# Dense channel-weight conversion, a later priority and a VectorE subtraction in an attention and token-mixing kernel

## The chip, the cores and the metric

The kernel runs on one core of a Trainium2 chip. Its time is device microseconds (us) of one execution. The core has five engines, each with a queue of its own that it works off in order: TensorE (PE in the profile; its weight loads are PEld), VectorE (DVE), ScalarE (ACT), GpSimd (POOL) and SyncE (SP), which here only starts transfers. Matmuls write to PSUM, and GpSimd works on SBUF alone in this kernel. The granted clock (PEclk) is the share of its full clock that TensorE was given.

## The reference

Batch 8, 8 heads, 576 positions, 64 values a head, 128 features. First an attention without a softmax over positions:

```
def phi(x):
    proj = einsum('bhsd,df->bhsf', x, w_phi)
    proj = proj - max(abs(proj), axis=-1)
    return concatenate([exp(proj), exp(-proj)], axis=-1)
kv  = einsum('bhsf,bhsd->bhfd', phi(k), v)
z   = sum(phi(k), axis=2)
out = einsum('bhsf,bhfd->bhsd', phi(q), kv) / (einsum('bhsf,bhf->bhs', phi(q), z) + 1e-6)
```

Its result, with the heads side by side as 512 channels, is `x` of a mixer, in float64 because the four weights are float64:

```
u   = x + (relu(xT @ w_tok1) @ w_tok2)T
out = u + relu(u @ w_ch1) @ w_ch2          # w_ch1 512 x 1536, w_ch2 1536 x 512
```

The maximum is per position, over the 128 features, for each of the 8 x 8 x 576 keys and queries.

## The kernel before

Heads are worked in 32 pairs `i` (4 for each batch). Six kinds of work are written as Python generators and woven together by `weave`:

- `keys` (for each pair five groups of key blocks): the projection `pp`, the maximum `mx`, the difference `pm`, both exponentials `kp`, then the sums `pkv` on TensorE.
- `queries` (for each pair a tail and four pieces): the same up to `pm`, then `turn` transposes on TensorE (`pt`), takes exponentials `qf`, splits them into a high and a low part (`qh`, `ql`), and `numerators` multiplies with `kv` (`pn`), inverts the denominators (`den`, a reciprocal on VectorE) and scales `xt` on GpSimd.
- `token_stream`: for each batch and each half of its channels transposes `px`, splits `xh`, `xl`, products `pa`, relu and split `ah`, `al`, products `ph`, and the sum into `xt`.
- `load_weights`: all weights are float64 in memory. `convert` loads one block as 64-bit words (`raw`), builds a float32 of it (`bits`) and splits that into two float32r parts. This takes one ScalarE instruction (an absolute value, L131), four on VectorE (L132 to L135), a rounding on ScalarE (L72) and a subtraction on GpSimd (L75). The 24 blocks of 128 x 512 of the channel weights are called `bitsc` in the profile; c1_c_e stands for block c of w_ch1 from column e on, c2_k for rows k of w_ch2.
- `channel_stream`: blocks of 256 positions, 18 in all. Block `i` takes six up projections `h` (L81) with relu and split `gh`, `gl`, and six down projections `acc`. It can start when the batch's tokens are mixed, and waits for the weights that it needs.

Products are made with float32r parts, three matmuls each (`mm3`, L79 to L82), but for batch 0 (pairs 0 to 3, `i < PLAIN`) keys and queries go through TensorE as float32, each such matmul showing as two records. There `less_max` is called with `base` 64 for keys and 0 for queries, and reads the projection straight from PSUM.

For base 0 (batch 0's queries) the maximum is negated on VectorE (`nmx`, L230) and added on ScalarE while it copies (L232, once for each block of 128 positions); in all other cases one subtraction (L234) does it, on VectorE for base 64, on GpSimd else.

What sets the order: `weave` always takes the next step of the stream that is behind its share. A step yields its cost, divided by the stream's share; the cost of a channel weight comes from `pace`, 8.0 until the queries of batch 0 are written out (pair 3 in `attended`), and then 1.0. The order in which instructions are written out is their priority for a scheduler, which then orders each engine's queue by what it reckons to be ready first. Steps of keys and queries are put ahead in it by `tc.high_priority()`, from the moment at which batch 0's token mix has been written out (`mixed` is not empty).

Of the kernel before, what the change touches and what calls it, by code (L numbers as in the profile page):

```python
# [12 lines left out]
AF = mybir.ActivationFunctionType  # L13
ALU = mybir.AluOpType
# [3 lines left out]
P = 128  # L18
B, H, S, D = 8, 8, 576, 64
NP = H // 2  # L20
F = 128
# [3 lines left out]
NC_, NE, NT = C // P, E // P, T // P  # L25
# [17 lines left out]
def mixer_kernel(ctx, tc, qk, vm, vt, w_phi, w1, w2, wc1, wc2d, out):  # L43
    nc = tc.nc

    cst = ctx.enter_context(tc.tile_pool(name="cst", bufs=1))
    wk = ctx.enter_context(tc.tile_pool(name="wk", bufs=2))
# [17 lines left out]
    def column(pool, n, **kw):  # L65

        return pool.tile([P, 32], F32, **kw)[:, :n]
# [71 lines left out]
        return t.rearrange("p a b -> p (a b)")  # L139

    def pace():
        return 1.0 if NP - 1 in attended else 8.0

    def load_weights():
        for u in (0, 3):
# [45 lines left out]
    def less_max(ts, units, name, base=None):  # L191

        n, kind = len(units), name[0]
        if base == D:
            ps = ps_a.tile([P, 2, 2, F], F32, tag=f"a{nplain['k'] % 2}", name=f"pp{name}")
            nplain["k"] += 1
        elif base == 0 and (nplain["q"] % 2 == 0 or nplain["q"] >= BORROWED):
            ps = ps_h.tile([P, 2, 2, F], F32, tag="h", name=f"pp{name}")  # L200
            nplain["q"] += 1
        elif base == 0:
            ps = ps_w.tile([P, 2, 2, F], F32, tag="keys", name=f"pp{name}", bufs=1)
            nplain["q"] += 1
        elif kind == "k":
            ps = ps_w.tile([P, 2, 2, F], F32, tag="keys", name=f"pp{name}", bufs=1)
        else:
            ps = ps_w.tile([P, 2, 2, F], F32, name=f"pp{name}", **REST)
        for i, u in enumerate(units):
            t, c = (ts[1], 512) if u is None else (ts[u[0]], P * u[1])  # L210
            if base is None:
                nc.tensor.matmul(ps[:, i].rearrange("p two f -> p (two f)"), t[:, c:c + P],  # L212
                                 wp2.rearrange("p two f -> p (two f)"), start=True, stop=True)
            else:
                rows = slice(base, base + D)
                nc.tensor.matmul(ps[:, i, 0], t[rows, c:c + P], wp[rows], start=True, stop=True)
        if base is None:
            part = wk.tile([P, 2, F], F32, tag="part", name=f"part{name}")
            nc.scalar.copy(part[:, :n], ps[:, :n, 1])
            pr = wk.tile([P, 2, F], F32, tag="p", name=f"p{name}")  # L220
            nc.vector.tensor_tensor(pr[:, :n], ps[:, :n, 0], part[:, :n], op=ALU.add)
            pr, eng = pr[:, :n], nc.gpsimd
        else:
            pr, eng = ps[:, :n, 0], nc.vector
        mx = column(wk, 2, tag=f"mx{kind}", name=f"mx{name}")
        nc.vector.tensor_reduce(mx[:, :n], pr, axis=AX.X, op=ALU.max, apply_absolute_value=True)
        pm = wk.tile([P, 2, F], F32, tag=f"pm{kind}", name=f"pm{name}", bufs=1 if kind == "t" else 2)
        if base == 0:
            nmx = column(wk, 2, tag="nmx", name=f"nmx{name}")
            nc.vector.tensor_scalar(nmx[:, :n], mx[:, :n], -1.0, None, op0=ALU.mult)  # L230
            for i in range(n):
                nc.scalar.activation(pm[:, i], pr[:, i], AF.Identity, bias=nmx[:, i:i + 1])  # L232
        else:
            eng.tensor_tensor(pm[:, :n], pr, mx[:, :n].unsqueeze(2).to_broadcast([P, n, F]), op=ALU.subtract)  # L234
        return pm

    nplain = {"k": 0, "q": 0}
    raws, pairs, kvs, loaded = {}, {}, {}, set()
    asked, attended, mixed = set(), set(), set()
# [307 lines left out]
    def weave(streams):  # L547

        streams = [[g, share, urgent, 0.0] for g, share, urgent in streams]
        now = 0.0  # L550
        while streams:
            for s in sorted(streams, key=lambda s: s[3]) * 2:
                with tc.high_priority() if s[2] and mixed else nullcontext():
                    step = next(s[0], "end")
                if step is None:
                    continue
                now = max(now, s[3])
                if step == "end":
                    streams.remove(s)
                else:  # L560
                    s[3] = max(s[3], now - LAG) + max(step, 0.01) / s[1]
                break
            else:
                raise RuntimeError("every stream waits")

    weave([(keys(), 5.2, True), (queries(), 5.2, True), (token_stream(), 8.0, False),
           (load_weights(), 10.0, False), (channel_stream(), 19.5, False)])

# [41 lines left out]
```

## Time and profile before

| | |
|---|---|
| median of 3 runs | 1180.97 us (1180.92 to 1181.36) |
| span of the profiled execution | 1183.6 us, 2.6 us above that median |
| TensorE busy | 1137.6 us, 96% |
| VectorE busy | 867.1 us, 73% |
| ScalarE, GpSimd busy | 531.5 us, 587.1 us |
| mean granted clock | 0.975 |

The span of the profiled execution goes from its first to its last instruction, and no other time of that execution is given. Rows of the page are read by stage: slices of 29.6 us show in tenths how busy an engine is. A line number of a helper, such as L81 (a matmul), L74 and L75 (a split), covers many uses, so the names of the tiles tell what it is.

### The profile page before, as it was taken

To read this page: it belongs to the slowest core of one execution; us is meant where nothing else is said; L and a number is where in the kernel's file an instruction comes from. 1 tells how busy PE (TensorE), PEld (TensorE's weight loads), DVE (VectorE), ACT (ScalarE), POOL (GpSimd) and SP (SyncE) were. 2 spreads that over 40 slices of the span, in tenths; PEclk is the share of its full clock that TensorE was granted. 3 is DMA by queue.
4 is the path that set the end of the run, shared out by engine and by line. 5 is a ranking of instruction groups with operands and counts; after the bars stand their busy time and mean duration, and the time that the engine had idled before them with its cause. 6 is when DMAs were issued, how large, how long until landed. Compare 5 with 4: busy or idle time off the path is not lost.

```text
span 1183.6 us, 24087 instructions
## 1 busy us (share of the span) xinstructions
PE 1137.6 (96%) x9032; PEld 1102.0 (93%) x9032; DVE 867.1 (73%) x1782; ACT 531.5 (45%) x1545; POOL 587.1 (50%) x734
## 2 busy tenths in 40 slices
PE   8789897899999999999999999999999999999998
PEld 7667887898999999999999999999999999999998
DVE  7977899986777888887878677684787978763111
ACT  5767565453444445444444443343353544431110
POOL 3344775854555566465555455473564655431000
PEclk9679898999999999999999999999999999999999
DMA  9541222111111111111111011110111110000000
GB/s 232 150 135 28 72 84 71 50 31 28 31 40 32 49 31 32 49 32 49 32 34 46 20 31 49 30 50 1 49 31 49 32 48 12 19 1 19 19 19 19
DMA packets 65300, 54.31 MB, mean 46 GB/s; under 512 B 44768, under 2 KB 56416, under 8 KB 65184
## 3 DMA queue, kind: packets, MB, share of 16 engines
q1 hardware_dynamic: 63824, 52.41, 15.4%
q8 instruction: 72, 1.18, 0.4%
q10 hardware_dynamic: 1360, 0.36, 0.2%
q14 instruction: 44, 0.36, 0.1%
HBM read 43.32 MB, written 9.44 MB: 45 GB/s over the span
## 4 chain that ended last, share of the span: by engine, by line
PE 78%; DVE 11%; ACT 4%; issue 3%; POOL 2%; DMA 2%; SPq 0%; DVEq 0%; POOLq 0%; ACTq 0%
PE h L81 23%; PE acc L81 23%; PE pkv L300 8%; PE pn L81 7%; PE ph L81 3%; PE pa L81 3%; PE pt L356 3%; PE ppq L212 2%; PE ppk L212 2%; DVE qh L74 2%; PE pn L389 1%; DVE den L401 1%; PE px L423 1%; DMA rawc<-in_wc 1%; DVE bitsc L132 1%
## 5 line engine op out<-in xcount | busy, mean ns | idle before, releaser
L81 PE MATMUL acc<-gh,wc 128*128 128x256 f32 x1728 | 345.1, 283 | 0.0
L81 PEld LDWEIGHTS acc<-gh,wc 128*128 128x128 f32 x1728 | 276.0, 188 | 0.2 <-ACT gh L489 0.2
L81 PE MATMUL h<-uh,wc_h 128*128 128x256 f32 x864 | 246.8, 286 | 4.3 <-ACT wc_h L72 2.2
L81 PE MATMUL h<-uh,wc_l 128*128 128x256 f32 x864 | 245.9, 285 | 0.8 <-POOL wc_l L75 0.8
L81 PE MATMUL h<-ul,wc_h 128*128 128x256 f32 x864 | 243.9, 282 | 0.3 <-POOL ul L470 0.3
L81 PE MATMUL acc<-gl,wc 128*128 128x256 f32 x864 | 242.0, 282 | 0.6 <-DVE gl L490 0.6
L278 ACT ACTIVATE kp<-pmk 128x256 f32<-128x256 f32 (+1 forms) x320 | 109.2, 389 | 171.1 <-POOL pmk L234 168.1
L300 PE MATMUL pkv<-v,kp 128*128 128x65 f32 (+1 forms) x1152 | 165.7, 278 | 6.8 <-ACT kp L278 3.3
L81 PEld LDWEIGHTS h<-uh,wc_h 128*128 128x128 f32 x864 | 163.7, 190 | 5.8 <-ACT wc_h L72 2.6
L300 PEld LDWEIGHTS pkv<-v,kp 128*128 128x128 f32 x1152 | 155.9, 200 | 12.6 <-ACT kp L278 5.4
L75 POOL TENSOR_TENSOR ql<-qf,qh 128x320 fp32r<-128x320 f32 (+1 forms) x112 | 103.4, 923 | 127.7 <-DVE qh L74 110.8
L81 PEld LDWEIGHTS h<-uh,wc_l 128*128 128x128 f32 x864 | 163.4, 189 | 1.1 <-POOL wc_l L75 1.1
L81 PEld LDWEIGHTS h<-ul,wc_h 128*128 128x128 f32 x864 | 163.8, 190 | 0.5 <-POOL ul L470 0.5
L81 PEld LDWEIGHTS acc<-gl,wc 128*128 128x128 f32 x864 | 162.5, 188 | 0.7 <-DVE gl L490 0.7
L490 DVE SCALAR_TENSOR_TENSOR gl<-h,gh 128x512 fp32r<-128x512 f32 x108 | 73.5, 680 | 89.2 <-ACT gh L489 88.7
L74 DVE CAST qh<-qf 128x320 fp32r<-128x320 f32 (+1 forms) x224 | 106.5, 489 | 34.6 <-ACT qf L363 29.1
L401 DVE RECIPROCAL den<-den 128x320 f32<-128x320 f32 x64 | 124.6, 1947 | 3.2 <-ACT den L397 2.2
L363 ACT ACTIVATE qf<-pt 128x320 f32<-128x320 f32 (+1 forms) x256 | 92.6, 412 | 71.2 <-PE pt L356 68.5
L81 PE MATMUL pn<-qh,kv 128*128 128x320 f32 (+1 forms) x448 | 118.8, 302 | 3.5 <-DVE qh L74 1.5
L489 ACT ACTIVATE gh<-h 128x512 fp32r<-128x512 f32 x108 | 64.9, 601 | 116.0 <-PE h L81 115.2
L402 POOL TENSOR_TENSOR xt<-xt,den 128x320 f32<-128x320 f32 x64 | 53.7, 839 | 114.7 <-DVE den L401 87.8
L470 POOL TENSOR_TENSOR ul<-xt,uh 128x64 fp32r<-128x64 f32 (+3 forms) x120 | 62.2, 543 | 84.2 <-ACT uh L469 83.3
(110 smaller groups left out, 2415.3 us busy)
## 6 DMA issues: line engine op xcount, KB each, us to landing
raw<-in_qk SPq DMA_DIRECT2D x27, 576.0 KB, 3.7
rawc<-in_wc SPq DMA_DIRECT2D x24, 512.0 KB, 4.2
v<-in_vm SPq DMA_DIRECT2D x31, 256.0 KB, 3.3
out_x<-xt SPq DMA_DIRECT2D x12, 256.0 KB, 2.2
out_x<-xt SPq DMA_DIRECT2D x16, 192.0 KB, 2.0
raw<-in_w SPq DMA_DIRECT2D x8, 256.0 KB, 4.6
out_x<-xt SPq DMA_DIRECT2D x16, 128.0 KB, 1.9
pair<-in_qk SPq DMA_DIRECT2D x8, 160.0 KB, 4.7
```

Source lines behind the costliest of these rows:

```text
L74: eng_hi.tensor_copy(hi, raw)
L75: eng_lo.tensor_tensor(lo, raw, hi.bitcast(F32), op=ALU.subtract)
L81: nc.tensor.matmul(o, a, m, start=first and i == 0, stop=last and i == 2, skip_group_check=group_ok)
L212: nc.tensor.matmul(ps[:, i].rearrange("p two f -> p (two f)"), t[:, c:c + P], wp2.rearrange("p two f -> p (two f)"), start=True, stop=True)
L278: nc.scalar.activation(kp[:, :len(us), sg], pm[:, :len(us)], AF.Exp, scale=1.0 - 2.0 * sg)
L300: nc.tensor.matmul(o, kp[:, n, sg], v, start=g == 0 and n == 0 and sg == 0, stop=u is None, skip_group_check=True)
L363: nc.scalar.activation(full, src, AF.Exp, scale=1.0 - 2.0 * sg)
L401: nc.vector.reciprocal(den, den)
L402: nc.gpsimd.tensor_tensor(x, x, den, op=ALU.mult)
L470: nc.gpsimd.tensor_tensor(l[:, d:d + n], t[:, c, o:o + n], h[:, d:d + n].bitcast(F32), op=ALU.subtract)
L489: nc.scalar.activation(gh, ph, AF.Relu)
L490: nc.vector.scalar_tensor_tensor(gl, ph, 0.0, gh.bitcast(F32), op0=ALU.max, op1=ALU.subtract)
```

## The change

Three edits:

- after batch 0's queries are written out, a channel weight's step costs 0.2 in place of 1.0 in the weave;
- keys and queries are put ahead from the moment at which the last channel weight's conversion is written out (`NE - 1 in loaded`), in place of the moment at which batch 0 is mixed;
- the branch for base 0 is gone, so that batch 0's queries are subtracted on VectorE out of PSUM, by the line that the keys use.

```diff
     def pace():
-        return 1.0 if NP - 1 in attended else 8.0
+        return 0.2 if NP - 1 in attended else 8.0
...
         pm = wk.tile([P, 2, F], F32, tag=f"pm{kind}", name=f"pm{name}", bufs=1 if kind == "t" else 2)
-        if base == 0:
-            nmx = column(wk, 2, tag="nmx", name=f"nmx{name}")
-            nc.vector.tensor_scalar(nmx[:, :n], mx[:, :n], -1.0, None, op0=ALU.mult)
-            for i in range(n):
-                nc.scalar.activation(pm[:, i], pr[:, i], AF.Identity, bias=nmx[:, i:i + 1])
-        else:
-            eng.tensor_tensor(pm[:, :n], pr, mx[:, :n].unsqueeze(2).to_broadcast([P, n, F]), op=ALU.subtract)
+        eng.tensor_tensor(pm[:, :n], pr, mx[:, :n].unsqueeze(2).to_broadcast([P, n, F]), op=ALU.subtract)
...
             for s in sorted(streams, key=lambda s: s[3]) * 2:
-                with tc.high_priority() if s[2] and mixed else nullcontext():
+                with tc.high_priority() if s[2] and NE - 1 in loaded else nullcontext():
                     step = next(s[0], "end")
```

The change moves instructions on every engine up to the end of channel block 1; on TensorE all that follows (7059 rows of 8352) stands in the same order as before. Three places show how. Lines behind the removed branch have numbers lower by 6 in the changed kernel. A name's first number is the pair (`pk`, `mx`, `den`), the batch (`al`, `xl`, `xt`) or the channel block (`h`, `acc`), and its last one only tells tiles apart.

VectorE, at the end of the token mix of batch 0's first half (`al0_0`), before:

```order
L226 TENSOR_REDUCE mxk4_1_978<-pk4_1_976 128x2
L401 RECIPROCAL den3_0_944<-den3_0_944 128x320
L75 TENSOR_TENSOR xl0_0_4_1036<-px0_0_4_1032,xh0_0_4_1035 128x256
L221 TENSOR_TENSOR pk4_2_1050<-ppk4_2_1045,partk4_2_1048 128x256
L226 TENSOR_REDUCE mxk4_2_1052<-pk4_2_1050 128x2
L449 SCALAR_TENSOR_TENSOR al0_0_1087<-pa0_0_930,ah0_0_1086 128x512
```

The same place in the changed kernel:

```order
L226 TENSOR_REDUCE mxk4_1_928<-pk4_1_926 128x2
L133 TENSOR_SCALAR bitsc1_2_1024_1546<-bitsc1_2_1024_1546 128x512
L221 TENSOR_TENSOR pk4_2_997<-ppk4_2_992,partk4_2_995 128x256
L133 TENSOR_SCALAR bitsc1_3_1024_1556<-bitsc1_3_1024_1556 128x512
L134 SCALAR_TENSOR_TENSOR bitsc1_1_1024_1536<-rawc1_1_1024_1534,bitsc1_1_1024_1536 128x512
L134 SCALAR_TENSOR_TENSOR bitsc1_2_1024_1546<-rawc1_2_1024_1544,bitsc1_2_1024_1546 128x512
L75 TENSOR_TENSOR xl0_0_4_983<-px0_0_4_979,xh0_0_4_982 128x256
L226 TENSOR_REDUCE mxk4_2_999<-pk4_2_997 128x2
L134 SCALAR_TENSOR_TENSOR bitsc1_3_1024_1556<-rawc1_3_1024_1554,bitsc1_3_1024_1556 128x512
```

The conversions of w_ch1's last third now stand among the links of batch 0's mix and of pair 4's keys.

VectorE behind batch 0's second half and the first up projection of channel block 0 (`gl0_0`), before:

```order
L401 RECIPROCAL den4_1_1535<-den4_1_1535 128x256
L490 SCALAR_TENSOR_TENSOR gl0_0_1649<-h0_0_1623,gh0_0_1648 128x512
L132 TENSOR_SCALAR bitsc2_4_1707<-bitsc2_4_1707 128x512
L221 TENSOR_TENSOR pq5_01_1833<-ppq5_01_1828,partq5_01_1831 128x256
L221 TENSOR_TENSOR pk6_2_1910<-ppk6_2_1905,partk6_2_1908 128x256
L74 CAST qh5_000_1804<-qf5_000_1802 128x320
L133 TENSOR_SCALAR bitsc2_4_1707<-bitsc2_4_1707 128x512
```

The same place in the changed kernel:

```order
L395 RECIPROCAL den4_1_1605<-den4_1_1605 128x256
L132 TENSOR_SCALAR bitsc2_11_1629<-bitsc2_11_1629 128x512
L221 TENSOR_TENSOR pk6_1_1845<-ppk6_1_1840,partk6_1_1843 128x256
L484 SCALAR_TENSOR_TENSOR gl0_0_1762<-h0_0_1736,gh0_0_1761 128x512
L133 TENSOR_SCALAR bitsc2_11_1629<-bitsc2_11_1629 128x512
L221 TENSOR_TENSOR pq5_01_1859<-ppq5_01_1854,partq5_01_1857 128x256
```

Before, the conversion of c2_4 begins here, with eleven to follow; now the last one of all, c2_11, stands here.

TensorE at the fifth up projection of channel block 0 (`h0_4`), before:

```order
L81 MATMUL h0_4_2188<-uh0_1_1609,wc1_h_90 128x256
L81 MATMUL h0_4_2188<-ul0_1_1610,wc1_h_90 128x256
L81 MATMUL acc0_1_1622<-gh0_3_2032,wc2_7_1894 128x256 x2
L81 MATMUL acc0_1_1622<-gl0_3_2033,wc2_7_1894 128x256
L81 MATMUL acc0_1_1622<-gh0_3_2032,wc2_7_1894 128x256
L81 MATMUL pa1_0_2299<-xl1_0_1_2341,w1_h_86 128x256
L81 MATMUL pa1_0_2299<-xh1_0_1_2340,w1_l_87 128x256
```

The same place in the changed kernel:

```order
L294 MATMUL pkv7_2385<-v1_97,kp7_1_2361 128x65 x4
L81 MATMUL acc0_0_1734<-gh0_3_2058,wc2_6_1461 128x256
L81 MATMUL acc0_1_1735<-gh0_3_2058,wc2_6_1461 128x256
L81 MATMUL h0_4_2154<-uh0_0_1702,wc1_h_90 128x256
L81 MATMUL h0_4_2154<-ul0_0_1703,wc1_h_90 128x256
L81 MATMUL h0_4_2154<-uh0_0_1702,wc1_l_91 128x256
```

Before, the 24 matmuls of `h0_4` are spread among down projections and batch 1's token mix; now they follow each other in one piece, and so do those of `h0_5`.

## The prediction

> **What bounds the kernel now.** I read the page's first two parts, then the windows view, then the timeline at two seams that the windows named.
>
> ```profile
> span 1183.6 us, 24087 instructions
> PE 1137.6 (96%) x9032; PEld 1102.0 (93%) x9032; DVE 867.1 (73%) x1782; ACT 531.5 (45%) x1545; POOL 587.1 (50%) x734
> PE   8789897899999999999999999999999999999998
> DVE  7977899986777888887878677684787978763111
> PEclk9679898999999999999999999999999999999999
> ```
>
> TensorE is busy for 96% of the span, and its row is full from slice 9 on. What it does not use lies in the first eight or nine slices (29.6 us each), where its granted clock is low as well. VectorE's row is fullest just there. The windows view (columns: busy time and count for PE, PEld, DVE, ACT, POOL, then granted clock, DMA share, GB/s) gives this by stage:
>
> ```profile
> 0.00:30.00 30.00, 26.02 (x108) 22.32 (x108) 23.58 (x63) 17.27 (x46) 9.29 (x22) 1.00 0.93 231
> 30.00:60.00 30.00, 23.93 (x111) 18.69 (x111) 29.30 (x53) 22.20 (x57) 10.15 (x9) 0.66 0.51 152
> 60.00:138.60 78.60, 70.50 (x405) 57.66 (x404) 60.72 (x121) 53.00 (x158) 40.66 (x41) 0.85 0.25 73
> 138.60:150.00 11.40, 10.93 (x74) 10.71 (x73) 10.25 (x21) 6.66 (x19) 7.93 (x11) 0.81 0.28 92
> 150.00:240.00 90.00, 78.02 (x587) 74.47 (x586) 85.72 (x149) 49.30 (x130) 58.83 (x61) 0.94 0.22 67
> 240.00:275.60 35.60, 35.60 (x304) 35.40 (x304) 24.46 (x48) 15.18 (x47) 19.77 (x27) 1.00 0.10 26
> 275.60:1183.60 908.00, 892.63 (x7457) 882.79 (x7455) 633.06 (x1334) 367.87 (x1090) 440.44 (x566) 1.00 0.11 32
> ```
>
> I cut at 138.6 and 275.6 us for two reasons. At 138.6 us VectorE finishes `al` of the second half of batch 0's token mix, and TensorE goes on with `ph` from it; at 275.6 us TensorE ends the down projection of channel block 1.
>
> ```profile
> 137.93 0.67 DVE L449 SCALAR_TENSOR_TENSOR al<-pa,ah 128x512 fp32r<-128x512 f32 x1
> 138.66 0.64 PE L81 MATMUL ph<-w_h,al 128*128 128x320 f32 x1
> 275.59 0.28 PE L81 MATMUL acc<-gh,wc 128*128 128x256 f32 x1
> ```
>
> From the second seam on, the order of TensorE's instructions is the same before and after the change, and up to it both kernels hold the same matmuls. So the change is worth what it does to the time of the second seam, 275.6 us. The 908.0 us behind it I carry over.
>
> Three stages stand ahead of it. From 30 to 60 us VectorE is the limit (29.30 of 30.00). From 60 to 138.6 us neither is: VectorE idles 78.60 − 60.72 = 17.9 us, and TensorE is slow (clock 0.85). From 150 to 240 us VectorE is the limit again (85.72 of 90.00), and TensorE loses 90.00 − 78.02 = 12.0 us idle and some clock. One place shows what it waits for:
>
> ```profile
> 195.00:200.00 5.00, 2.24 (x8) 1.84 (x9) 4.83 (x9) 2.60 (x6) 1.40 (x2) 0.76 0.48 131
> 200.00:205.00 5.00, 5.00 (x27) 5.00 (x26) 4.76 (x10) 3.30 (x8) 3.28 (x4) 0.55 0.20 79
> PE h L81 <- ACT wc_h L72: 2.2, 1, 2.2
> ```
>
> Channel block 0 wants a weight that is still being converted, and the idle time is followed by a stretch at 0.55 of the clock.
>
> **Pace and priority: what moves.** The two edits to the weave have one effect. Before, 12 of the 24 channel weights are converted on VectorE behind the second `al`; in the changed order 11 of these 12 stand ahead of it, between batch 0's third and fourth pair and batch 1's first keys. One (the last, wc2_11) stays behind. The price of a conversion on VectorE is four instructions, in the windows of the tile `bitsc` (columns: DVE, ACT, POOL, clock, DMA, GB/s):
>
> ```profile
> 30.00:75.00 45.00, 31.11 (x46) 12.36 (x20) 14.00 (x10) 0.66 0.51 155
> 150.00:222.00 72.00, 37.95 (x48) 14.57 (x23) 14.48 (x11) 0.93 0.21 64
> ```
>
> That is 31.11 / 46 × 4 = 2.71 us early and 37.95 / 48 × 4 = 3.16 us late, so 11 cost 29.8 to 34.8 us. I take 2.8 us, near the early price, so 30.8 us: between 85 and 112 us GpSimd has 10.36 of 27 us to do, little as in the early stage, where it holds 10.15 of 30.00.
>
> ```profile
> 60.00:85.00 25.00, 21.90 (x106) 16.74 (x106) 20.90 (x39) 16.58 (x48) 11.73 (x9) 0.73 0.44 141
> 85.00:112.00 27.00, 25.18 (x139) 20.05 (x138) 16.45 (x31) 19.96 (x61) 10.36 (x10) 0.87 0.13 35
> 112.00:138.60 26.60, 23.42 (x165) 20.87 (x163) 23.37 (x52) 16.46 (x51) 18.57 (x22) 0.95 0.18 48
> ```
>
> The same row shows the hole into which they go: 27.00 − 16.45 = 10.6 us of idle VectorE, with 4.1 us before it and 3.2 us behind.
>
> The conversions' other instructions move along. On ScalarE (an `Abs` and a rounding, 14.57 / 23 × 2 = 1.3 us each) 11 make 14 us, for which 78.60 − 53.00 = 25.6 us are idle, and the third edit takes work off it. On GpSimd (one subtraction, 14.48 / 11 = 1.3 us) 14 us go into 78.60 − 40.66 = 37.9 us. Both I cost at nothing; without that cover they would hold up batch 0's `kp` and `qf` on ScalarE by up to 14 us. On SP, 11 weight DMAs now stand ahead of the loads of pairs 5 and 6. A weight DMA lands in 4.2 us but waits for its staging tile:
>
> ```profile
> rawc<-in_wc SPq DMA_DIRECT2D x24, 512.0 KB, 4.2
> SPq L125 <- DVE bitsc L135: 39.9, 9, 11.8
> ```
>
> What queues behind it is the load of `raw6`, for which the stacking of pair 6's keys waits on VectorE. Bounds: nothing, to one landing of 4.2 us; I take nothing, because VectorE has conversions in front of that stacking.
>
> **The subtraction.** For the 16 two-block and 4 one-block query units of batch 0, a negation on VectorE and one or two biased copies on ScalarE become one subtraction on VectorE out of PSUM. The keys do this already, so there is a row for it:
>
> ```profile
> L234 DVE TENSOR_TENSOR pmk<-ppk,mxk 128x256 f32<-128x256 f32 x16 | 6.6, 412 | 0.2
> L234 DVE TENSOR_TENSOR pmk<-ppk,mxk 128x128 f32<-128x128 f32 x4 | 1.1, 278 | 0.0
> L230 DVE TENSOR_SCALAR nmxq<-mxq 128x2 f32<-128x2 f32 x16 | 6.7, 417 | 0.0
> L230 DVE TENSOR_SCALAR nmxq<-mxq x16: 152/158/1240, 9.4 to 103.8; 128x2 f32<-128x2 f32 x16
> L232 ACT ACTIVATE pmq<-ppq,nmxq 128x128 f32<-128x128 f32 x32 | 10.1, 366 | 4.7 <-DVE nmxt L230 3.0 <-DVE nmxq L230 1.5
> ```
>
> Added: 6.6 + 1.1 = 7.7 us. Removed: 6.7 us by the mean, which holds a few long ones (up to 1240 ns), or 16 × 0.158 = 2.5 us by the median, and 0.6 us for the four small ones (taken at about the same 0.14 to 0.16). So VectorE gains between 0.4 and 4.6 us of work; I take 2.0, since part of the long ones was a stall that moves to the next instruction. ScalarE loses 10.1 us and some more for the tails, off a limit nowhere.
>
> The Trainium skill's page "SBUF — State Buffer", section "Who interferes with whom", says that a VectorE instruction with at most one SBUF input, outside the two-port modes, does not contend with GpSimd. By that the subtraction holds at 412 ns wherever it stands, as its row does; the same section has conversions contend, and by it they would be priced at the late 3.16 us once GpSimd is fuller, 4 us more than my 2.8 us gives.
>
> **The sum.** Time of the second `al`: VectorE's busy time up to it, 23.58 + 29.30 + 60.72 = 113.6 us; plus conversions 30.8; plus subtractions 2.0; plus idle time. Of the idle time the 7.1 us of the first 60 us stay. Of the 17.9 us behind that I keep 3.5, since the conversions need only a DMA and ScalarE, and stand between the links of batch 0's chain. Together 157.0 us, 18.4 us later than before.
>
> From there TensorE has 74 + 587 + 304 = 965 matmuls to the second seam. In the stage that loses nothing they take 35.60 / 304 = 0.1171 us apiece, so 113.0 us; before, they took 275.6 − 138.6 = 137.0 us, 24.0 us more. VectorE's share behind the `al` falls from 10.25 + 85.72 + 24.46 = 120.4 us to 120.4 − 37.95 + 3.2 = 85.7 us, so it no longer sets the pace. The loss left there I bound by nothing (240 to 275.6 us) and by the long stage behind, 892.63 busy but 908.00 / 7457 = 0.1218 us a matmul: 965 × 0.0047 = 4.5 us. I take 2.0.
>
> 157.0 + 113.0 + 2.0 = 272.0 us against 275.6: 3.6 us earlier. The profiled span would be 1180.0 us. That execution is 2.6 us longer than the median of the plain runs, 1180.97 us, so I take the difference over: **1177.4 us**, 0.3% faster.
>
> **Rivals.** *It cancels.* With conversions at 3.05 us and 4 us of idle kept, the `al` comes at about 160.5 us, and 160.5 + 113.0 + 2.0 = 275.5 us: 1181 us. For it speaks GpSimd's 18.57 of 26.60 us from 112 to 138.6 us, against it the emptier stretch before that.
>
> *Batch 0's chain waits behind conversions (slower).* VectorE works in order, and its waits in the early stage are for TensorE:
>
> ```profile
> DVE mxq L226 <- PE ppq L216: 10.0, 4, 3.2
> ```
>
> If these links stay as long as they are, since TensorE is slow between 30 and 138.6 us, an idle stretch is no hole that a conversion of fixed place can fill. With 10 of the 17.9 us kept and 3.1 us a conversion, the `al` comes at 113.6 + 34.1 + 3.0 + 7.1 + 10 = 167.8 us, the seam at 282.8: 7.2 us slower, 1188 us. It decides from an `al` later than about 163 us. Against it: in the changed order the last reciprocal of pair 1 comes ahead of conversions (c1_1_512 to c1_3_512) that stood before it, so TensorE is fed sooner there.
>
> The clock sharpens this rival: TensorE's row has 0.66 where it is busy 23.93 of 30.00 us, and in the changed kernel it has 18 us more idle before the `al`. The Trainium skill's page "TensorE: Matmul & The Clock Gate", section "HAM oscillation — how this bites in real kernels", says that one idle window of some 3.4 us brings the half clock back. By that rule the 11.4 us behind the `al` run at 0.81 again, which is in the 2.0 us of loss that I kept.
>
> *It does not do what it says.* If the order alone moved but VectorE's stalls stayed in place, only the subtraction would show: 0.4 to 4.6 us on VectorE where it is the limit, most of it hidden later; no change.
>
> **How the numbers follow.** A measurement of this kernel can tell about 0.2%, 2.4 us, from no change. Forecast, faster: 0.42. Cancelled, or without effect: 0.27. Chain behind conversions: 0.31. The ends: conversions at the early 2.71 us, subtraction at 0.4 and no idle kept give an `al` at 150.9 and a seam at 263.9 us, 11.7 us faster, 1169 us; the late price, 4.6 us and all idle kept an `al` at 178.0 and 295.5 us, 20 us slower. The last is far out; I set 1170 to 1189, which leaves about one in ten on either side. The forecast's own range is 1170 to 1178.6.
>
> **What would show it.** Right: `bitsc` has nearly nothing on VectorE behind the second `al`; that `al` ends near 157 us; from it to the end of channel block 1's down projection pass 113 to 118 us at a clock of 1.00; VectorE idles under 5 us between 60 us and the `al`; no `h` waits for `wc_h`. Wrong: an `al` later than 163 us, or a stretch behind it above 120 us with waits for `ql`, `qh` or `pmq`, or a tail behind the seam that is not 908 us.

## The result: slower, with the second `al` at 163 us and not at 157

The changed kernel takes 1191.89 us (median of 4 runs, 1188.45 to 1192.8) where the kernel before, run beside it, takes 1180.95 us (4 runs, 1180.44 to 1181.36): a ratio of 1.0081, 95% interval 1.0061 to 1.0100, 10.9 us slower. I had forecast 1177.4 us, faster, and a range that ended at 1189. The profiled execution took 1191.87 us, so it stands for the plain runs.

The page of the changed kernel, the lines that answer to those shown of before (PEclk is the granted TensorE clock in tenths):

```profile
span 1190.0 us, 24058 instructions
PE 1143.0 (96%) x9032; PEld 1106.6 (93%) x9032; DVE 862.0 (72%) x1782; ACT 525.0 (44%) x1509; POOL 586.9 (49%) x734
PE   8987689999999999999999999999999999999998
DVE  7899997576777888787878677584787978763111
PEclk9667799999999999999999999999999999999999
```

TensorE's clock now sags in slices 2 to 5 (29.8 to 148.8 us, digits 6, 6, 7, 7) where it sagged in slices 2 to 7 before (6, 7, 9, 8, 9, 8): for a shorter time, but deeper. The windows of the changed kernel, cut at the same two seams (columns: busy time and count for PE, PEld, DVE, ACT, POOL, then granted clock, DMA share, GB/s):

```profile
0.00:30.00 30.00, 26.18 (x115) 22.24 (x115) 22.29 (x60) 14.80 (x36) 9.33 (x21) 1.00 0.90 220
30.00:60.00 30.00, 27.32 (x114) 20.28 (x113) 25.75 (x46) 20.98 (x54) 8.35 (x7) 0.68 0.42 130
60.00:163.30 103.30, 80.73 (x396) 66.25 (x395) 97.48 (x173) 61.29 (x156) 61.53 (x54) 0.76 0.35 101
163.30:280.00 116.70, 114.76 (x959) 113.85 (x960) 83.73 (x172) 59.59 (x174) 67.26 (x87) 1.00 0.13 38
280.00:1190.00 910.00, 893.97 (x7454) 883.97 (x7452) 632.79 (x1334) 368.30 (x1090) 440.38 (x566) 1.00 0.11 32
```

The seams themselves, from the timeline (start, duration, instruction):

```profile
162.68 0.67 DVE L443 SCALAR_TENSOR_TENSOR al<-pa,ah 128x512 fp32r<-128x512 f32 x1
163.41 0.42 PE L81 MATMUL ph<-w_h,al 128*128 128x320 f32 x1 [0.21 <-DVE al L443]
279.69 0.28 PE L81 MATMUL acc<-gh,wc 128*128 128x256 f32 x1
```

And the conversions (tile `bitsc`; columns DVE, ACT, POOL, clock, DMA, GB/s):

```profile
80.00:163.30 83.30, 41.58 (x54) 16.40 (x26) 21.21 (x15) 0.78 0.33 96
163.30:185.00 21.70, 2.23 (x4) 1.28 (x2) 1.30 (x1) 1.00 0.13 48
```

The change does what it says. Behind the second `al` one conversion is left (2.23 us of VectorE), no `h` waits for `wc_h`, and the stretch to the second seam shrank from 137.3 to 116.7 us at a clock of 1.00. But the `al` moved from 138.6 to 163.3 us. The seam came 4.1 us later (that matmul ends at 280.0 us and ended at 275.9; the 275.6 us of the prediction is its start), not 3.6 us earlier.

### The profile page after: what moved, and what is told of

Same layout as the page of the kernel before. It is cut to its first block, busy times and chain, and to the rows that moved or that the text cites. A ratio compares the mean times of both kernels' runs of the same rounds, so it can differ in the third digit from the quotient of the medians.

```text
span 1190.0 us, 24058 instructions
## 1 busy us (share of the span) xinstructions
PE 1143.0 (96%) x9032; PEld 1106.6 (93%) x9032; DVE 862.0 (72%) x1782; ACT 525.0 (44%) x1509; POOL 586.9 (49%) x734
## 4 chain that ended last, share of the span: by engine, by line
PE 79%; DVE 12%; ACT 3%; POOL 3%; issue 2%; DMA 1%; DVEq 0%; POOLq 0%; ACTq 0%
PE acc L81 24%; PE h L81 23%; PE pkv L294 9%; PE pn L81 7%; PE pa L81 3%; PE ph L81 3%; PE pt L350 2%; PE ppq L212 2%; PE ppk L212 2%; DVE den L395 2%; DVE qh L74 2%; PE px L417 1%; DVE bitsc L134 1%; PE pn L383 1%; PE ppk L216 1%
## 5 line engine op out<-in xcount | busy, mean ns | idle before, releaser
L294 PE MATMUL pkv<-v,kp 128*128 128x65 f32 (+1 forms) x1152 | 169.4, 282 | 8.6 <-ACT kp L272 5.9
L294 PEld LDWEIGHTS pkv<-v,kp 128*128 128x128 f32 x1152 | 159.9, 204 | 14.9 <-ACT kp L272 9.0
L75 POOL TENSOR_TENSOR ql<-qf,qh 128x320 fp32r<-128x320 f32 (+1 forms) x112 | 103.4, 923 | 141.1 <-DVE qh L74 122.0
L81 PEld LDWEIGHTS h<-uh,wc_l 128*128 128x128 f32 x864 | 162.5, 188 | 0.0
L228 POOL TENSOR_TENSOR pmk<-pk,mxk 128x256 f32<-128x256 f32 (+1 forms) x140 | 84.5, 603 | 36.2 <-DVE mxk L226 35.8
```

Of the source, the lines that this page charges most:

```text
L75: eng_lo.tensor_tensor(lo, raw, hi.bitcast(F32), op=ALU.subtract)
L81: nc.tensor.matmul(o, a, m, start=first and i == 0, stop=last and i == 2, skip_group_check=group_ok)
L294: nc.tensor.matmul(o, kp[:, n, sg], v, start=g == 0 and n == 0 and sg == 0, stop=u is None, skip_group_check=True)
```

## Experiments

Each ratio is to the kernel before, run on the same chip beside it, with its 95% interval. "Second `al`", "seam" and "rest" are read from the profiled execution: the end of `al` of batch 0's second half, the end of channel block 1's down projection, and the span from there.

### The kernel before once more

Edit: none, a second profile of the kernel before.

> The kernel before, unchanged. It is run because the profiled execution of it has a span of 1183.6 us, 2.6 us above the median of its plain runs, while the profiled execution of the changed kernel is as long as its plain runs. If that first profile was unusually long, this one has a span near 1179 us, and the second seam (end of channel block 1's down projection) lies near 271 us in place of 275.6; the 24 us that TensorE loses behind the second al are then 20 or less. If it was usual, span 1183.6 us and seam 275.6 us come again.

```profile
span 1180.3 us, 24087 instructions
60.00:135.60 75.60, 66.99 (x418) 54.92 (x416) 61.10 (x124) 54.79 (x162) 40.48 (x41) 0.95 0.27 79
135.60:272.60 137.00, 124.28 (x960) 120.34 (x961) 120.60 (x217) 71.17 (x196) 86.77 (x98) 0.95 0.20 59
272.60:1180.30 907.70, 892.45 (x7455) 882.44 (x7453) 633.36 (x1334) 368.25 (x1090) 441.16 (x566) 1.00 0.11 32
```

The second `al` stands at 135.6 us and the seam at 272.6, each about 3 us ahead of the profile on which I worked; the two stretches behind are equal within 0.3 us. So that profile was of a long execution, and its excess lay ahead of the `al`. An execution's time goes with its granted clock: of 19 runs of the kernel before on one chip, the 14 at a mean clock of 0.980 or more took 1179.0 to 1182.5 us, the 5 at 0.974 to 0.977 took 1186.1 to 1187.9 us. On the four other chips the first kind took up to 1185.0 us, the second 1184.6 us or more.

### The parts alone, and the whole again

The subtraction alone (three times, on three occasions), the weave alone (twice; its second edit is inert: with a pace of 0.2 all engines have the same order of instructions with and without the priority edit), the whole twice more, and a pace of 0.6. Edits against the kernel before:

```diff
-        if base == 0:
-            nmx = ...
-        else:
-            eng.tensor_tensor(pm[:, :n], pr, ...)
+        eng.tensor_tensor(pm[:, :n], pr, ...)        # the subtraction alone
```

```diff
-        return 1.0 if NP - 1 in attended else 8.0
+        return 0.2 if NP - 1 in attended else 8.0    # the weave alone; 0.6 in the third kernel
-                with tc.high_priority() if s[2] and mixed else nullcontext():
+                with tc.high_priority() if s[2] and NE - 1 in loaded else nullcontext():
```

> The third edit alone: batch 0's queries are subtracted on VectorE, 12 conversions stay behind the second al as before. Theory 'conversions delay the al': VectorE has 0.4 to 4.6 us more work up to the al, so al at 139 to 144 us, seam later by 0 to 4 us, time +0 to +4 us. Rival 'the subtraction carries it' (it also changes VectorE's order in the first 90 us): time +5 us or more, the larger part of the 10.9 us.

> The first two edits without the third: 11 conversions ahead of the second al, batch 0's queries as before (negation on VectorE, copies on ScalarE). Theory 'conversions delay the al': al at 157 to 165 us, seam at al + 113 to 118 us, time +5 to +11 us. Rival 'the subtraction carries it': time within 3 us of before.

> Pace 0.6 in place of 1.0, priority as in the change, no third edit: only 3 conversions (15 in place of 12) stand ahead of the second al. Theory 'the hole takes what fits': 3 x 2.8 = 8.4 us of VectorE work go into 17.9 us of idle time, al at 139 to 144 us, and VectorE has 8 us less behind it in the stage where it is the limit: time -1 to -7 us. Rival 'each conversion ahead of the al delays it by its full price': al at 147 us, seam between 1 us earlier and 4 us later, time -1 to +4 us.

> The changed kernel once more, beside the kernel before on one chip. The parts alone came 6.2 us (subtraction) and 3.3 us (weave) later than the kernel before. If the two costs are separate they add: 9 to 11 us slower, with the second al at 161 to 165 us and its seam at 278 to 282 us. If both pay with the same wait (the half-clock stretch ahead of 90 us) they overlap: 5 to 8 us slower, second al at 157 to 161 us.

> The subtraction alone once more. Theory 'its order of work costs it': the ratio to the kernel before is 1.003 to 1.007 again, and the half-clock time from 55 us to the second al is over 20 us also where TensorE reaches the full clock by 32 us. Rival 'the late first full clock of that execution': the ratio is 0.999 to 1.003, with the full clock reached by 32 us and the al at 136 to 140 us.

> The subtraction alone in five rounds beside the other two. Theory 'its order costs it' (VectorE idle 10 to 12 us in the first 60 us rather than 7.5): ratio 1.002 to 1.004. Rival 'it costs nothing that can be told': 0.999 to 1.002. Above 1.004 the first measurement holds and not the second.

> The weave alone in five rounds beside the other two. By 1.0023 before: ratio 1.001 to 1.0035.

> The whole change in five rounds beside its parts. Theory 'the parts add': its excess over 1 is that of the two beside it together, within 0.15%. Rival 'the whole costs more than its parts' (VectorE has no idle time left to take the subtraction's later tiles): 1.006 to 1.009, over 0.15% above the sum of the two.

| kernel | ratio | second `al` | `al` to seam | seam | rest |
|---|---|---|---|---|---|
| before (2 profiles) | 1 | 138.6, 135.6 | 137.3, 137.0 | 275.9, 272.6 | 907.7, 907.7 |
| subtraction, first | 1.0052 [1.0037, 1.0067] | 146.2 | 133.2 | 279.4 | 909.9 |
| subtraction, second | 1.0013 [0.9993, 1.0032] | 139.2 | 136.1 | 275.3 | 909.8 |
| subtraction, third | 1.0040 [1.0022, 1.0058] | 141.1 | 135.9 | 277.0 | 909.9 |
| weave, first | 1.0023 [1.0010, 1.0035] | 159.9 | 117.3 | 277.2 | 908.6 |
| weave, second | 1.0022 [1.0009, 1.0036] | 156.7 | 117.3 | 274.0 | 908.7 |
| pace 0.6 | 1.0029 [1.0011, 1.0046] | 137.6 | 138.4 | 276.0 | 907.0 |
| whole, again | 1.0068 [1.0045, 1.0091] | 161.7 | 116.6 | 278.3 | 910.5 |
| whole, third | 1.0081 [1.0060, 1.0101] | 162.5 | 116.7 | 279.2 | 909.9 |

The third subtraction, the second weave and the third whole ran on one chip in five rounds; here are their windows from 60 us to the second `al`, then from the `al` to the seam, in this order:

```profile
60.00:141.10 81.10, 73.25 (x394) 61.12 (x394) 64.83 (x124) 48.28 (x138) 44.38 (x45) 0.78 0.28 82
141.10:277.00 135.90, 122.53 (x950) 118.47 (x949) 116.28 (x213) 70.88 (x191) 83.30 (x96) 0.95 0.19 56
```

```profile
60.00:156.70 96.70, 78.63 (x395) 62.62 (x394) 91.63 (x160) 63.37 (x175) 55.97 (x50) 0.77 0.29 93
156.70:274.00 117.30, 115.69 (x968) 114.84 (x968) 86.51 (x179) 60.36 (x179) 68.76 (x89) 1.00 0.14 41
```

```profile
0.00:30.00 30.00, 26.04 (x108) 22.00 (x108) 22.27 (x60) 14.61 (x35) 9.25 (x21) 1.00 0.84 215
30.00:60.00 30.00, 25.59 (x132) 19.97 (x130) 28.18 (x52) 21.46 (x55) 8.34 (x7) 0.82 0.49 153
60.00:162.50 102.50, 81.89 (x386) 66.70 (x385) 94.96 (x166) 60.81 (x155) 61.63 (x54) 0.70 0.33 97
162.50:279.20 116.70, 114.82 (x959) 113.91 (x960) 83.70 (x172) 59.63 (x174) 67.36 (x87) 1.00 0.13 37
```

What follows. Both parts cost time, and on that one chip they come to 0.40% + 0.22% = 0.62% against 0.81% for the whole: within the intervals they add, and the rival "the whole costs more than its parts" is not separated from it.

The weave alone fills VectorE ahead of the `al` (91.63 of 96.70 us) and empties it behind, as meant. Its `al` is 21 us late, the stretch behind it 20 us shorter: they cancel, and 1 us of the rest is lost too.

The subtraction alone leaves all 12 late conversions where they were. Its `al` comes 5 us later on average (142.2 us in three profiles, 137.1 in two of before), and the rest is 2.2 us longer in all three. VectorE has somewhat more to do up to the `al` (114.6, 115.3 and 117.2 us in the three, against 113.6 and 112.1 before). I had explained the first measurement by idle time in the first 60 us (17.0 us against 9.0 in the repeat of before); the second and third profile have 9.8 and 7.7 us there, so that reading falls: it belonged to that one execution, in which TensorE reached the full clock only at 53 us. Between 55 us and the `al` the three profiles spend 37.5, 37.5 and 41.0 us at the half clock (25.6 and 13.0 in the two of before), and the ratios do not follow it. The size of this part stays between 0.1 and 0.5%, and its cause open.

Pace 0.6 put three conversions into the hole ahead of the `al` at no cost there (137.6 us), earlier than the 139 to 144 us that I had expected; but the stretch behind did not shrink (138.4 us), and the time was 0.3% longer where I had expected 1 to 7 us less. It is not simply a smaller dose of the weave: TensorE's order differs from that of the kernel before beyond the seam as well (only the last 6063 rows agree, 7059 in the whole). Why the stretch did not shrink stays open.

### Is it the half clock? Matmuls added inside the half-clock stretches

In all these kernels TensorE falls to half its clock for stretches ahead of the seam. To see whether that is a cause, I put matmuls that nobody reads ahead of the transposes of one query tile; the transposes overwrite their result.

```diff
     def turn(i, k, j, pm, tail):
         ...
+        if (i, k, j) in [(1, 0, 0)]:      # (1, 1, 1) with the subtraction alone, and in the whole with 16
+            for _ in range(32):           # 16 in others
+                nc.tensor.matmul(ptr..., wp2[:, 0], wp2..., start=True, stop=True)
         for n, r in enumerate(rows):
             nc.tensor.transpose(ptr[:, n], r, ident)
```

> The subtraction alone, and 32 matmuls of one weight tile against itself (128x256, float32r, their result is overwritten) ahead of the transposes of batch 1's last query tile, about 65 us, right behind the point where TensorE fell to the half clock in the run of the subtraction alone and stayed there for 34 us. They are extra work: 3.8 us at the granted clock 1.00, 6.8 us at 0.50, by 0.117 us of one. Theory 'the half clock carries it' (VectorE waits for keys and queries that TensorE makes at the half clock): the clock is back at 1.00 by about 75 us and not at 97 us, the second al ends at 137 to 143 us and not at 146.2, the time is 0 to 6 us below that of the subtraction alone. Rival 'the order carries it' (the new order of tiles makes VectorE wait, whatever the clock): the second al ends at 146 to 153 us, the time is 0 to 7 us above that of the subtraction alone.

> The changed kernel with the same 32 matmuls ahead of the transposes of the first query tile of batch 1's first pair, about 43 us, inside the stretch from 40.7 to 71.4 us that it ran at the half clock. Theory 'the half clock carries it': the stretch ends by about 53 us, the second al ends at 155 to 161 us and not at 163.3, the time is 1 to 7 us below that of the changed kernel. Rival 'the order and the conversions carry it': the second al ends at 163 to 170 us, the time is 0 to 7 us above that of the changed kernel.

> The kernel before with the same 32 matmuls ahead of the transposes of the first query tile of batch 1's first pair, about 55 us, where it ran at the half clock from 50.9 to 61.1 us and from 68.0 to 74.8 us. Theory 'the half clock carries it': the second of these stretches goes or both shorten, the second al ends at 131 to 135 us and not at 135.6, the time is 0 to 4 us below the kernel before. Rival 'the order carries it': the al ends at 136 to 142 us, the time is 0 to 7 us above.

By their `al` all three runs with 32 met the theory 'the half clock carries it' (138.0, 160.1 and 133.8 us). But with 32 of them the order that the scheduler finds changes behind the place (some 170 of VectorE's 1782 rows in the kernel before). So I took two controls: 16 matmuls, with which VectorE, GpSimd and SyncE keep their order and ScalarE and TensorE move a few rows, and 16 float32 matmuls of 128x128 (`wp` times `wp`), with which all engines have the order of the 32.

> The subtraction alone with 16 float32r matmuls rather than 32 at the place of the burst before. With 32 the order of the work behind changes too (about 175 of VectorE's 1784 rows move); with 16 VectorE, GpSimd and SyncE keep the order of the subtraction alone row for row, and ScalarE moves 3 rows by a place. Theory 'clock': the 16 end the half-clock stretch that they stand in (1.9 to 3.4 us of work), the second al ends at 137 to 143 us, the time is 0.2 to 0.8% below that of the subtraction alone (ratio to the kernel before 0.997 to 1.003). Rival 'order' (the gain of the 32 came from the new order behind them): the al ends at 146 to 150 us, ratio 1.005 to 1.009. A ratio as high with a clock that does not come back says that 16 are too few to tell.

> The subtraction alone with 16 matmuls of float32 128x128 at the same place: all engines then have the order of the run with 32 float32r matmuls row for row, and only the type of the filler differs; by eight pkv matmuls of 65 columns in 1.00 us they last about 4 us at the granted clock 1.00 and 8 at 0.50. Theory 'clock', if float32 work does not bring the clock back: the half-clock stretch goes on past the filler, al 144 to 152 us, ratio to the kernel before 1.003 to 1.010. Rival 'order': the al ends at 136 to 142 us and the ratio is 0.997 to 1.002, as with the 32 float32r. If the clock comes back here too, the run does not tell the two apart, and shows that float32 work in one block wakes it.

> The kernel before with 16 float32r matmuls at the place of the burst that made it 0.6% faster with 32. VectorE, GpSimd and SyncE keep the order of the kernel before row for row. Theory 'clock': the half-clock stretch about 50 us ends in or behind the 16, and the ratio to the kernel before is 0.993 to 0.998. Rival 'order': ratio 1.000 to 1.004 (16 matmuls of work and no gain).

> The kernel before with 16 float32 matmuls of 128x128 at that place: row for row the order of the run with 32 float32r matmuls on all engines. Theory 'clock', if float32 work does not bring the clock back: ratio 0.999 to 1.006. Rival 'order': ratio 0.992 to 0.997, as with 32 float32r (0.9941).

> The changed kernel with 16 float32r matmuls ahead of the transposes of batch 1's last query tile (59 to 62 us), the place where 16 of them took the cost of the subtraction alone away; VectorE, GpSimd and SyncE keep the changed kernel's order row for row. Theory 'the half clock carries the subtraction's share here too': the first half-clock stretch ends by about 63 us and not at 71 to 72, the second al ends at 154 to 159 us and not at 162 to 163, the ratio to the kernel before is 1.001 to 1.004. Rival 'with the weave VectorE sets the al' (its idle time from 60 us to the al is only some 6 us): the stretch ends early as well, but the al ends at 160 to 164 us and the ratio is 1.005 to 1.010.

> The weave alone with 16 float32r matmuls ahead of the transposes of the first query tile of batch 1's first pair (53 us), inside its half-clock stretch from 41.0 to 61.4 us; VectorE, GpSimd and SyncE keep the weave's order row for row. Theory 'the half clock carries the weave's cost': the stretch ends by about 56 us, the second al ends at 154 to 158 us and not at 159.9, the ratio to the kernel before is 0.997 to 1.000. Rival 'VectorE sets the al': al 159 to 163 us, ratio 1.001 to 1.005.

| kernel | no filler | 16, same order | 32, new order | 16 float32, the same new order |
|---|---|---|---|---|
| before | 1 | 1.0007 [0.9989, 1.0025] | 0.9941 [0.9925, 0.9958] | 0.9953 [0.9938, 0.9968] |
| subtraction | 1.0052, 1.0013, 1.0040 | 1.0006 [0.9988, 1.0024] | 0.9992 [0.9970, 1.0014] | 0.9992 [0.9975, 1.0008] |
| weave | 1.0023, 1.0022 | 1.0011 [0.9992, 1.0030] | | |
| whole | 1.0081, 1.0068, 1.0081 | 1.0055 [1.0036, 1.0075] | 1.0073 [1.0040, 1.0107] | |

The filler brings the full clock back where it stands. In the kernel before with 32 of them (first 50.1 us, last 55.7 us) the clock is back at 54.0 us, inside the filler:

```profile
37.00:50.00 13.00, 9.71 (x32) 7.45 (x31) 13.00 (x24) 8.44 (x21) 4.49 (x5) 0.50 0.43 119
50.00:54.00 4.00, 4.00 (x19) 3.91 (x18) 4.00 (x7) 3.29 (x9) 1.14 (x2) 0.50 0.46 133
54.00:60.00 6.00, 6.00 (x51) 5.32 (x50) 5.76 (x12) 3.48 (x10) 3.19 (x3) 1.00 0.33 111
```

Yet with an unchanged order it wins nothing in the kernel before, and 0.1 to 0.5% in the others; of these only the first measurement of the subtraction stands apart by its interval. These runs settle less than I meant them to, since a stretch that ends sooner does not always leave less time at the half clock. The median of the mean granted clock, over all runs of a kernel (without filler: 117 of the kernel before, 24, 20 and 14 of the others), shows it; it leaves out the start, ahead of the first clock record:

| kernel | no filler | 16, same order | 32, new order | 16 float32, the same new order |
|---|---|---|---|---|
| before | 0.981 | 0.980 | 0.991 | 0.989 |
| subtraction | 0.978 | 0.986 | 0.987 | 0.987 |
| weave | 0.975 | 0.976 | | |
| whole | 0.971 | 0.979 | 0.976 | |

In the kernel before and in the weave the 16 did not raise it: in the profile of the first the half clock came back from 62.7 to 83.2 us. These two runs say nothing of what the half clock costs. In the subtraction they raised it, the `al` came at 137.5 us and the ratio fell to 1.0006, as the theory 'clock' had it; beside the 1.0013 of the same chip without filler this is no difference that can be told.

In the whole, a half-clock stretch that began at 63.2 us ended at 66.7, inside the filler, where that of the changed kernel lasts until 71 to 73 us in three profiles. The `al` did not come sooner (165.7 us). That profile is of a long execution, which reached the full clock only at 53 us, with VectorE idle for 15.8 of the first 60 us; from 60 us on VectorE is busy for 100.60 of the 105.70 us up to the `al` and sets it.

```profile
60.00:165.70 105.70, 82.66 (x425) 68.51 (x424) 100.60 (x181) 64.99 (x165) 62.28 (x55) 0.77 0.34 99
```

The whole's ratio, 1.0055 against 1.0068 to 1.0081, is lower, but the intervals overlap, and the filler's own 3.8 us of TensorE stand in it. So what the half clock carries of the whole's 0.8% is not shown. The stretches between 80 and 152 us stayed; there VectorE is the one that is full, and the half clock looks like its consequence. What they cost was not measured by itself.

The gain of the 32 in the kernel before is another matter: 1174.82 us, faster than both kernels, with 5.9 us of useless work in it. Here are the windows of that kernel, then of the float32 control, then of the 16 in the old order, each from the second `al` to the seam and, for the first two, on to the end:

```profile
133.80:267.30 133.50, 121.93 (x969) 117.38 (x970) 118.03 (x219) 73.14 (x198) 90.14 (x99) 0.99 0.20 60
267.30:1173.60 906.30, 892.34 (x7444) 882.59 (x7443) 632.82 (x1331) 368.08 (x1088) 438.61 (x565) 1.00 0.11 32
```

```profile
136.40:270.60 134.20, 123.52 (x969) 118.62 (x970) 118.59 (x219) 73.38 (x198) 89.47 (x99) 0.97 0.21 60
270.60:1177.10 906.50, 892.49 (x7445) 882.63 (x7443) 633.14 (x1331) 368.33 (x1088) 439.40 (x565) 1.00 0.11 32
```

```profile
136.70:274.10 137.40, 125.06 (x962) 120.95 (x961) 120.79 (x217) 71.27 (x196) 86.39 (x98) 0.95 0.19 59
```

The gain goes with the order, not with the kind of filler: about 3 us less from the `al` to the seam and about 1 us less behind it (906.3 and 906.5 us against 907.2 to 907.7 in the old order). Without the control I would have put these 0.6% down to the matmuls themselves. The clock is not ruled out by it. In the float32 controls the full clock came back as well (at 50.6 and 62.0 us), so by what I had written ahead they do not part clock and order. The new order has the higher one (0.991 and 0.989 against 0.980), from the `al` to the seam too (0.99 and 0.97 against 0.95), and whether it wins through that was not separated. The new order without any filler was not tried.

## Why the prediction was wrong

| term (us) | predicted | profile of the result | whole, again | third whole |
|---|---|---|---|---|
| VectorE busy up to the second `al` | 146.4 | 22.29 + 25.75 + 97.48 = 145.5 | 146.2 | 145.4 |
| VectorE idle, first 60 us | 7.1 | 12.0 | 8.9 | 9.6 |
| VectorE idle, 60 us to the `al` | 3.5 | 5.8 | 6.6 | 7.5 |
| second `al` | 157.0 | 163.3 | 161.7 | 162.5 |
| `al` to seam | 115.0 | 116.7 | 116.6 | 116.7 |
| rest | 908.0 | 910.0 | 910.5 | 909.9 |
| span | 1180.0 | 1190.0 | 1188.8 | 1189.1 |

Set as means against the two profiles of before, the `al` of the whole is 25.4 us later, the stretch behind it 20.5 us shorter and the rest 2.4 us longer: 7.3 us in all.

**Where it held.** VectorE's work was priced right as a sum. A conversion came to 41.58 / 54 × 4 = 3.1 us rather than 2.8, and the busy sum is still within a microsecond; in the weave alone it is 144.2 and 143.1 us where my sum without the 2.0 us has 144.4. So 2.8 us held as what moving a conversion adds. The subtraction took its row's time (411 ns, as the keys), so nothing showed of a contention with GpSimd. The stretch behind the `al` came within 1.7 us, with the clock of 1.00 that I named.

**The step that failed** is the idle time in "The sum": "the 7.1 us of the first 60 us stay" and "of the 17.9 us behind that I keep 3.5". They were 12.0 and 5.8 us, 8.9 and 6.6, 9.6 and 7.5 in the three profiles: 5 to 7 us more than the 10.6 I kept. That alone turns −3.6 into +1 to +4. Against the means of both profiles of before, VectorE's work up to the `al` grew by 32.9 us, as I had it (32.8), but its idle time fell by 7.5 us and not by 14.4. Some of this is the base: the repeat of before idles 9.0 us in its first 60, so 7.1 was the figure of one execution. What VectorE waits for in the changed kernel, up to 60 us and then from 60 to 160 us (the waits view: engine, line, what it waited for, us in total, times, longest):

```profile
DVE mxk L226 <- PE ppk L216: 7.2, 3, 5.1
DVE bitsc L132 <- ACT bitsc L131: 2.5, 2, 1.5
DVE mxt L226 <- PE ppk L216: 1.1, 1, 1.1
```

```profile
DVE xl L75 <- ACT xh L72: 2.0, 1, 2.0
DVE mxk L226 <- PE ppk L216: 1.2, 1, 1.2
DVE mxq L226 <- PE ppq L216: 0.6, 1, 0.6
```

Of the first row one wait of 5.1 us is not new: both profiles of before have it at the start (5.2 and 5.3 us). The wait of `bitsc` for its own step on ScalarE and that of `xl`, a link of batch 0's mix, are new: before has no such row of `bitsc` in these 60 us, and 0.2 us of `xl` at most behind them.

The 10.0 us of waiting for `ppq` that I had shown behind 60 us (5.6 us in the repeat) did go, to 0.6. This does not show that conversions filled the hole: in the subtraction alone, which moves none, the wait is 0.4 to 1.8 us as well. And the two waits for ScalarE come with the subtraction. Here is the subtraction alone, first profile, up to its `al`, and then the weave alone, second profile, from 60 us to its `al`:

```profile
DVE xl L75 <- ACT xh L72: 4.8, 3, 2.0
DVE bitsc L132 <- ACT bitsc L131: 2.3, 2, 1.5
```

```profile
DVE mxq L226 <- PE ppq L216: 1.2, 1, 1.2
DVE pq L221 <- ACT partq L219: 1.0, 2, 0.8
DVE mxk L226 <- PE ppq L216: 0.7, 1, 0.7
```

The weave alone has neither of the two waits, but many small ones. It idles 15.7 and 13.6 us up to its `al` in its two profiles, 3 to 5 us more than 10.6, so that the `al` stands at 159.9 and 156.7 us where my own sum without the 2.0 us gives 155.0. So the miss has two parts: the moved conversions do not use the idle time up to the last 3.5 us, and the third edit brings waits for ScalarE, that of `xl` on batch 0's chain itself, where I had only seen that ScalarE loses work. I had counted what leaves a hole and not what the new order opens. Why ScalarE comes later with the third edit stays open.

**The second miss** is the rest. I carried 908.0 us over (907.7 from the end of that matmul) because TensorE's order there is the same. It is 910 us in the whole and in the subtraction alone, 908.7 in the weave alone. TensorE's busy time grows from 892.63 to 893.97 us. In the whole and in the subtraction alone 0.5 to 1.3 us of the excess lie between the ends of channel blocks 5 and 6, and 0.3 us behind the last block; what is left is spread. I did not find its cause.

**The third** is the start. The profiled execution of before lay further above its plain runs than the 2.6 us that I set: a run's time is 2.2 us above its span (1182.49 against 1180.3 in the repeat), so the span to set beside 1183.6 was 1180.95 − 2.2 = 1178.8. I took the difference over as it was, while the changed kernel's profile is at its median. The gap between −3.6 and +10.9 us is 14.5: 8.0 from the seam (280.0 against 272.0), 2.0 from the rest, and 4.5 from this.

**The rivals.** "Batch 0's chain waits behind conversions" is the one that came, at the edge of its own deciding point: an `al` at 161.7 to 163.3 us. Its idle time came as a sum, 15.5 to 17.8 us against its 17.1, but not where it had it: behind 60 us VectorE kept 5.8 to 7.5 us, between my 3.5 and its 10, and in the first 60 us 8.9 to 12.0, where both had 7.1. Its price of 3.1 us a conversion is what the row gives, but the sum of VectorE's work came out by my 2.8. It had the seam 2.8 us too late (282.8 us), and its 1188 us lacked the longer rest and the correction for the long profile: errors that cancel in part, so that its coming close is in part luck. "It cancels" describes the weave alone rather well (1.002). The trace agrees with the Trainium skill's page "TensorE: Matmul & The Clock Gate", section "HAM oscillation — how this bites in real kernels", in that the clock falls where TensorE idles ahead of the `al` (0.76, and 0.70 in another execution), but no single idle window of 3.4 us was needed for it: ahead of the seven half-clock stretches of the changed kernel the longest idle time in 3.4 us was 0.8 to 2.0 us. That the 11.4 us behind the `al` would run at 0.81 again did not come true, they ran at 1.00.

## What to carry to other kernels

When work is moved into an engine's idle time, look for the waits that the new order opens (links that now come later, other engines that answer later), not only for those that it closes, and read each edit's waits from a run of that edit alone. Set the profiled execution beside the plain runs by its span before a difference of a few microseconds is carried over, and take a second profile where a few tenths of a per cent are at stake. Where a scheduler sets the order, every edit also reshuffles the work, which was worth nearly as much here (0.6%) as the whole change (0.8%): judge an added instruction beside a control with the same order.

## What the runs showed of the hardware

TensorE starts at the half clock, and the granted-clock column does not say so. In the repeat of before the windows give 1.00 from 10 to 28 us and from 28 to 47 us, TensorE busy throughout, but the same two forms of matmul take 741 ns by median there and 432 ns later (the groups of `pn` by window, the last three columns of durations being min, median, max):

```profile
10.00:28.00 18.00, 18.00 (x78) 15.33 (x76) 17.20 (x45) 11.98 (x35) 5.09 (x5) 1.00 0.91 230
28.00:47.00 19.00, 19.00 (x69) 15.15 (x69) 18.86 (x36) 14.20 (x36) 7.71 (x6) 1.00 0.65 178
```

```profile
L389 PE MATMUL pn<-qf,kv x12: 634/741/900, 28.0 to 45.8; 128*128 128x320 f32 x8, 128*128 128x256 f32 x4
L389 PE MATMUL pn<-qf,kv x28: 377/432/537, 85.9 to 108.8; 128*128 128x256 f32 x16, 128*128 128x320 f32 x12
```

By form, the 128x320 matmuls of this group take 741 ns ahead of the first clock record, 741 ns in stretches recorded at 0.50 and 433 ns at 1.00 (medians). The first record of a full clock came at 27 to 31 us in 16 of the 20 profiles, and at 47 to 53 us in the other four; the column shows 1.00 ahead of the first record. I had read the first 30 us as full speed. Every half-clock stretch lasted a multiple of 3.41 us (3.4, 6.8, 10.2, 13.7, 17.1, 20.5, 30.7, 34.1).

The stretches follow how full TensorE's row is, with no long gap needed. Ahead of each of the 13 half-clock stretches in the first profiles of the kernel before and of the change, the row was filled to 0.10 to 0.85 for 3.41 us, with gaps of 2.0 us at most; the last 3.41 us of each were filled to 0.91 to 1.00. At the start a full row did not do: in the repeat of before it was full from 10 to 47 us, 37 us, at the half clock.

With a block of dense matmuls added, the full clock was back 1.1 to 4.5 us after its first one in all nine profiles, float32 as well as float32r (the float32 block from 58.1 us on ended, at 62.0 us, a half-clock stretch that began at 58.6; the float32r block from 50.1 us ended one at 54.0).
